# Attention and two gated layers on one core: a batch's sums inverted as 84 rows of 64 columns, re-laid through DRAM

## The chip, the cores and the metric

The kernel runs on one core of one Trainium2 chip. The metric is the time of one execution on the device, in microseconds (us). The engines are named as in the profile: PE (TensorE, matmuls; PEld are its weight loads), DVE (VectorE), ACT (ScalarE), POOL (GpSimd) and SP (SyncE, which issues nearly all DMAs, in the order of the program). A lower time is better.

## The reference

Attention over 4 batches of 12 heads, 448 positions and 64 columns a head, with scores capped by a tanh, and behind it two layers over 1792 tokens of 768 columns:

```python
scores = cap * np.tanh(scale * np.matmul(q, k.T) / cap)
attn = np.exp(scores - max);  attn = attn / (np.sum(attn, axis=-1) + 1e-09)
x = (attn @ v) as [B * S, H * D]
h = x @ w_in;   x = (h - np.tanh(h)) @ w_out
h = x @ w_in2;  x = (h / (1 + np.exp(-1.702 * h))) @ w_out2
```

The part that matters here is the division by the sums: 4 x 12 x 448 numbers are inverted, and each result multiplies 64 columns of a head's output.

## The kernel before

Attention takes the heads in pairs: 24 steps `g`, six to a batch. Keys lie on the partitions, so the sums over keys come from PE: `key_adds` adds a pair's key blocks on DVE, `sums_of_two` (L582) multiplies by a 0/1 matrix and leaves in a PSUM tile `ps_r` the sums of four heads, one row in each group of 32 partitions. `add_sums` (L605) collects three of them in an SBUF tile `w` of 128 partitions and 448 columns, of which 12 rows hold sums. In the two steps that follow, `batch_recip` (L610) inverts `w` in place, one half of the columns in a step, over all 128 partitions, and then stores the 12 rows to a DRAM tensor `wrow` (L615), which is in two parts, since the layers take the tokens in two passes (768 and 1024). `w_rows` (L621) loads a row again, repeated over 64 partitions, for the multiplication by the inverse: in the first pass as tiles `wb`, multiplied in attention (L666); in the second pass from DRAM in `x_load`, much later.

A step on PE is: two score blocks (L526), the transposes of a later pair's q and k (`prep`, L505 and L514, into two PSUM tiles `ps_qk`), the next pair's first score block, then in even steps `ps_r`, in odd ones the tails of two pairs, and the products with v (L568). `ps_qk` and `ps_r` share two PSUM buffers (`ps_s`), so `ps_r` starts only when DVE has copied the first of the two `ps_qk` out to `qk` (L90), and a transpose starts only when `add_sums` has read `ps_r`. The order of the work on PE, DVE, ACT and POOL in attention is that of the code (`pin`). DMAs are not pinned: a scheduler puts them between each other on SP. They are the loads of q, k and v (L465 to L493), the weights of the first layer (`wd`, L189), their converted parts to and from DRAM (`kept`, L240, L316), the part of attention's output that the second pass takes (`xd`, L592), `wrow` and `wb`.

Attention ends with the last batch's two reciprocals, while PE is already in the first layer's product (`gemm_in`, L912, a generator of which the end of attention takes the first matmuls). The last reciprocal and the last exponential are `marks`: some conversions of weights are placed behind them.

Of the kernel before, what the change touches and what calls it, by code (L numbers as in the profile page):

```python
# [9 lines left out]
F32 = mybir.dt.float32  # L10
# [5 lines left out]
ALU = mybir.AluOpType  # L16
# [24 lines left out]
def attention_moe_moe(ctx, tc, q, k, v, cap, w_in1, w_out1, w_in2, w_out2, out):  # L41
    nc = tc.nc
    B, H, S, D = q.shape
# [33 lines left out]
    def pin(ins):  # L77
        return tc.keep_in_program_order(ins) if pinned[0] else ins
# [13 lines left out]
    def lo_dve(dst, src, hi):  # L92
        return pin(nc.vector.tensor_tensor(out=dst, in0=src, in1=hi.bitcast(F32), op=ALU.subtract))  # L93

    ident = const.tile([P, P], F32, name="ident")
    make_identity(nc, ident)
    capr = const.tile([P, 1], F32, name="capr")
    cpos = const.tile([P, 1], F32, name="cpos")
    tsc = const.tile([P, 1], F32, name="tsc")
    cub_a = const.tile([P, 1], F32, name="cub_a")  # L100
    cub_u = const.tile([P, 1], F32, name="cub_u")
    const.tile([P, 24], F32, name="pad")

    xa = [dr_p.tile([P, TOKENS[0]], F32, name=f"xa{i}") for i in range(KM)]
    xd = [dr_p.tile([P, TOKENS[1]], F32, name=f"xd{i}") for i in range(KM)]
    wrow = [dr_p.tile([4, NP // 2, n], F32, name=f"wrow{p}") for p, n in enumerate(TOKENS)]
    x_big = big.tile([P, 2 * KM * TOKENS[0]], F32R, name="x")
    xs_h, xs_l = ([[x_big[:, (m * KM + i) * n:(m * KM + i + 1) * n] for i in range(KM)] for n in TOKENS[:1]] for m in range(2))
    xh, xl = list(xs_h[0]), list(xs_l[0])
# [17 lines left out]
    ps_v = first_pool("ps_v", 2, space=bass.MemoryType.PSUM)  # L127

    SR = P // 4
    sel = one_p.tile([P, NP // 2, SR], F32, name="sel")  # L130
    vt = [one_p.tile([P, P], F32, name=f"vt{i}") for i in range(4)]

# [316 lines left out]
    def parts_of(b):  # L449
        parts = []  # L450
        for p, n in enumerate(TOKENS):
            a, z = max(b * S - FIRST[p], 0), min((b + 1) * S - FIRST[p], n)
            if a < z:
                parts.append((p, a, z))
        return parts
# [142 lines left out]
    def add_sums(g):  # L598
        b, p = divmod(g // 2, NP // 2)
        ps = sum_t.pop(g)[:, :S]  # L600
        if p == 0:
            w_t[b] = w_p.tile([P, S], F32, tag="w", name="w")
            hi_dve(w_t[b], ps)
        else:
            pin(nc.vector.tensor_tensor(out=w_t[b], in0=w_t[b], in1=ps, op=ALU.add))  # L605

    def batch_recip(b, half):
        a = slice(half * S // 2, (half + 1) * S // 2)
        w = w_t[b]
        ins = pin(nc.vector.reciprocal(out=w[:, a], in_=w[:, a]))  # L610
        if half:
            c = 0
            for p, a, z in parts_of(b):
                for n in range(4):
                    nc.sync.dma_start(out=wrow[p][n, :, a:z], in_=w[n * SR:n * SR + NP // 2, c:c + z - a])  # L615
                c += z - a
        return ins

    def w_rows(t, p, i, a, z):
        for j in range(2):  # L620
            nc.sync.dma_start(  # L621
                out=t[j * D:(j + 1) * D], in_=wrow[p][i % 2 * 2 + j, i // 2, a:z].partition_broadcast(D)
            )

    conv_at = [3, 5, 7, 9, 11, 14, 16, 18, 20]
# [2 lines left out]
    def attention():  # L628
        wb = {}

        def x_of(g):
            return [n for n, at in enumerate(split_at) if at == g]

        def x_part(n):
            b, i = divmod(n, NP)
            n = S if b == 0 else CUT
            return i, n, slice(b * S, b * S + n)

        load_qk(0, nc.scalar)
        nc.sync.dma_start(out=capr, in_=cap.partition_broadcast(P))  # L640
        nc.vector.tensor_scalar(
            out=cpos.bitcast(U32), in0=capr.bitcast(U32), scalar1=0x7FFFFFFF, scalar2=None, op0=ALU.bitwise_and
        )
        nc.vector.reciprocal(out=tsc, in_=cpos)
        nc.vector.tensor_scalar(out=tsc, in0=tsc, scalar1=QK_SCALE, scalar2=None, op0=ALU.mult)
        load_qk(1)
        load_v(0)
        load_qk(2)
        load_v(1)

        def prep(g):
            prep_q(g)
            prep_k(g)

        prep(0)
        scores(0, 0)
        prep(1)
        tail_scores(0)
        for g in range(NG):
            pair_act(g, (0, KC) if g % 2 == 0 else (0,))  # L660
            if g - 2 in conv_at:
                conv_hi(early[conv_at.index(g - 2)])
            for n in x_of(g):
                i, w, a = x_part(n)
                x = xs[n][:, :w]
                pin(nc.vector.tensor_tensor(out=x, in0=x, in1=wb.pop(n)[:, :w], op=ALU.mult))  # L666
                hi_pool(xh[i][:, a], x)
            scores(g, 1)
            scores(g, 2)
            last_exp = pair_act(g, (1, 2))  # L670
            if g + 1 in conv_at:
                conv_exp(early[conv_at.index(g + 1)])
            load_v(g + 2)
            if g in conv_at:
                conv_low(early[conv_at.index(g)])
            if g - 1 in conv_at:
                conv_or(early[conv_at.index(g - 1)])
            for n in x_of(g):
                i, w, a = x_part(n)
                lo_pool(xl[i][:, a], xs.pop(n)[:, :w], xh[i][:, a])  # L680
            if g - 2 in conv_at:
                conv_lo(early[conv_at.index(g - 2)])
            if g >= NP and g % NP < 3:
                b = g // NP - 1
                if g % NP:
                    batch_recip(b, g % NP - 1)
            for n in {0: (2,), 1: (3, 4)}.get(g, (g + 3,)):
                prep(n)
            for n in {0: (3, 4)}.get(g, (g + 4,)):
                load_qk(n)  # L690
            for n in x_of(g + 1):
                wb[n] = wb_p.tile([P, S], F32, tag="wb", name="wb")
                i, w, a = x_part(n)
                w_rows(wb[n][:, :w], 0, i, a.start, a.stop)
            if g in (1, 3):
                dbl_dma()
            if g == NG - 1:
                tail_pv(g - 1)
                pair_pv(g, 0)
                prepare(1)  # L700
                hold[0] = True
                for _ in range(12):
                    next(moe_0)
            scores(g + 1, 0)
            if g % 2:
                tail_scores(g + 1)
                if g < NG - 1:
                    tail_pv(g - 1)
            elif g:
                sums_of_two(g - 2)  # L710
            key_adds(g)
            if g % 2 == 0 and g:
                add_sums(g - 2)
            for c in range(1 if g == NG - 1 else 0, KC):
                pair_pv(g, c)
            if g % 2:
                pair_out(g - 1)
                pair_out(g)
        for _ in range(5):
            next(moe_0)  # L720
        hold[0] = False
        sums_of_two(NG - 2)
        add_sums(NG - 2)
        for half in range(2):
            rec = batch_recip(B - 1, half)
        marks.extend((last_exp.ins, rec.ins))


    late = []
# [162 lines left out]

    def gemm_in(layer):
        for f in f_order[layer]:
            if plain[0] and f == KF - 1:
                rate[0] = 0.0
            i, (wh, wl) = w_next()
# [446 lines left out]
```

## Time and profile before

| | us |
|---|---|
| runs | 1053.99, 1056.22, 1056.51 |
| median | 1056.22 |
| profiled execution | 1055.68 |
| its span, first to last instruction | 1053.9 |
| PE busy in the span | 1038.7 |
| DVE busy | 819.6 |
| ACT busy | 692.0 |
| POOL busy | 56.1 |

The profile is of one execution. Its span leaves out 1.8 us around the instructions. Busy time of PE is modelled at the ends of matmuls. A row of the timeline begins with its start and its length in us; equal instructions that follow each other are one row with a count, and in brackets stands the engine's idle time before the row and what ended it. On SP a row's length is the time in which it issued the DMAs, not that of the transfers.

### The profile page before, as it was taken

What the parts mean: (1) busy time and instruction counts of PE and PEld (TensorE: products, weight loads), DVE (VectorE), ACT (ScalarE), POOL (GpSimd) and SP (SyncE); (2) the same over time, 40 slices, a digit from 0 to 9 for tenths busy, and PEclk for the clock granted to TensorE, in tenths of its full rate; (3) what the DMA queues carried; (4) which work ended last, traced back from release to release, by engine and by line L of the source; (5) the groups of instructions that cost most, each with busy time, mean ns of one, the idle gap of its engine ahead of it and who ended that gap; (6) DMA issues with size and microseconds to landing.
All of it is one profiled execution on the core that took longest, in us unless ns stands there. A gap on an engine that the chain in (4) does not pass through costs nothing.

```text
span 1053.9 us, 15397 instructions
## 1 busy us (share of the span) xinstructions
PE 1038.7 (99%) x5483; PEld 857.8 (81%) x5483; DVE 819.6 (78%) x1097; ACT 692.0 (66%) x958; POOL 56.1 (5%) x56
## 2 busy tenths in 40 slices
PE   8999999999999999999999999999999999999998
PEld 3333333899999998888878888887899999999998
DVE  4799999899986517988899897685899974448973
ACT  6999898787854335556775757655755745557663
POOL 0123444100000000000000000000000000000000
PEclk9999999999999999999999999999999999999999
DMA  5777688765588958888673852898654554444443
GB/s 132 196 217 219 181 228 257 255 228 192 195 257 275 327 170 287 289 277 283 219 253 118 299 183 82 272 321 297 224 164 126 190 155 130 129 118 143 153 134 104
DMA packets 153749, 218.17 MB, mean 207 GB/s; under 512 B 58380, under 2 KB 101704, under 8 KB 153672
## 3 DMA queue, kind: packets, MB, share of 16 engines
q1 hardware_dynamic: 152376, 216.58, 64.9%
q8 instruction: 43, 0.70, 0.3%
q10 hardware_dynamic: 1296, 0.61, 0.2%
q14 instruction: 34, 0.28, 0.1%
HBM read 158.86 MB, written 58.28 MB: 206 GB/s over the span
## 4 chain that ended last, share of the span: by engine, by line
PE 81%; DVE 11%; ACT 3%; DMA 3%; issue 2%; SPq 0%; DVEq 0%; ACTq 0%
PE ps_o L1194 19%; PE ps_h L912 19%; PE ps_h L1092 19%; PE ps_y L952 9%; PE ps_y L1005 5%; PE ps_pv L568 3%; PE ps_sc L526 3%; DVE gr L361 1%; DVE wl L93 1%; ACT t L545 1%; DVE rl L93 1%; DVE ts L557 1%; PE ps_r L582 1%; DVE ts L556 1%; PE ps_tl L536 1%
## 5 line engine op out<-in xcount | busy, mean ns | idle before, releaser
L81 ACT CAST rh<-gr 128x512 fp32r<-128x512 f32 (+1 forms) x179 | 103.6, 584 | 99.7 <-PE ps_o L1194 63.2
L912 PE MATMUL ps_h<-x,wh 128*128 128x384 f32 (+1 forms) x672 | 153.0, 358 | 0.0
L93 DVE TENSOR_TENSOR rl<-gr,rh 128x512 fp32r<-128x512 f32 (+1 forms) x179 | 113.8, 642 | 25.8 <-ACT rh L81 25.1
L1194 PE MATMUL ps_o<-wh,rl 128*128 128x384 f32 x392 | 131.1, 334 | 0.0
L1194 PE MATMUL ps_o<-wh,rh 128*128 128x384 f32 x392 | 131.1, 334 | 0.0
L1194 PE MATMUL ps_o<-wl,rh 128*128 128x384 f32 x392 | 131.1, 334 | 0.0
L912 PEld LDWEIGHTS ps_h<-x,wh 128*128 128x128 f32 x672 | 121.1, 188 | 12.0 <-issue 0.7
L93 DVE TENSOR_TENSOR wl<-whole,wh 128x768 fp32r<-128x768 f32 (+1 forms) x103 | 94.0, 912 | 13.7 <-ACT wh L81 12.8
L81 ACT CAST wh<-whole 128x768 fp32r<-128x768 f32 (+1 forms) x103 | 82.4, 800 | 24.7 <-PE ps_h L1092 10.6
L1092 PE MATMUL ps_h<-x,wh 128*128 128x384 f32 (+1 forms) x336 | 97.3, 359 | 0.0
L912 PE MATMUL ps_h<-x,wl 128*128 128x384 f32 (+1 forms) x384 | 88.1, 364 | 0.0
L545 ACT ACTIVATE t<-ps_sc,tsc 128x896 f32<-128x896 f32 x72 | 69.8, 1005 | 15.1 <-PE ps_sc L526 15.0
L912 PEld LDWEIGHTS ps_h<-x,wl 128*128 128x128 f32 x384 | 69.8, 188 | 9.7 <-issue 1.4
L1194 PEld LDWEIGHTS ps_o<-wl,rh 128*128 128x128 f32 x392 | 73.6, 188 | 0.0
L1194 PEld LDWEIGHTS ps_o<-wh,rh 128*128 128x128 f32 x392 | 73.6, 188 | 0.0
L1194 PEld LDWEIGHTS ps_o<-wh,rl 128*128 128x128 f32 x392 | 73.6, 188 | 0.0
L547 ACT ACTIVATE t<-t,cpos 128x896 f32<-128x896 f32 x72 | 72.4, 1042 | 0.4
L526 PE MATMUL ps_sc<-qk 64*128 64x448 f32 x288 | 68.3, 568 | 2.3 <-ACT t L545 1.5
L361 DVE TENSOR_TENSOR gr<-gr 128x512 f32<-128x512 f32 (+2 forms) x112 | 69.3, 645 | 0.6 <-DMA gr<-xa 0.4
L361 DVE TENSOR_TENSOR part<-ps_h,part 128x512 f32<-128x512 f32 (+1 forms) x48 | 29.8, 621 | 51.3 <-PE ps_h L1092 51.1
L1092 PE MATMUL ps_h<-x,wl 128*128 128x512 f32 (+1 forms) x192 | 69.6, 362 | 0.0
L219 DVE SCALAR_TENSOR_TENSOR wr<-wr,wd 128x768 uint32<-128x768 uint32 x48 | 46.0, 961 | 28.4 <-ACT wd L211 20.7
(155 smaller groups left out, 2188.1 us busy)
## 6 DMA issues: line engine op xcount, KB each, us to landing
wd<-in_moe_w_in_dram SPq DMA_DIRECT2D x64, 384.0 KB
wd<-in_moe_w_out_dram SPq DMA_DIRECT2D x29, 768.0 KB
whole<-single SPq DMA_DIRECT2D x36, 384.0 KB
whole<-s SPq DMA_DIRECT2D x33, 384.0 KB
wh<-kept SPq DMA_DIRECT2D x25, 384.0 KB
wl<-kept SPq DMA_DIRECT2D x25, 384.0 KB
single<-wr SPq DMA_DIRECT2D x24, 384.0 KB
whole<-t SPq DMA_DIRECT2D x22, 384.0 KB
```

The source lines that it names most:

```text
L81: pin(nc.scalar.copy(out=dst, in_=src))
L93: return pin(nc.vector.tensor_tensor(out=dst, in0=src, in1=hi.bitcast(F32), op=ALU.subtract))
L219: pin(nc.vector.scalar_tensor_tensor(out=u, in0=u, scalar=3, in1=dbls.pop(i)[:, :, 0], op0=ALU.logical_shift_left, op1=ALU.bitwise_or))
L361: nc.vector.tensor_tensor(out=out, in0=a, in1=b, op=kind)
L526: pin(nc.tensor.matmul(ps[:, j, :S], qk[a, kc], qk[a, :S], start=True, stop=True))
L545: pin(nc.scalar.activation(out=t, in_=ps[:, :, :S], func=AF.Tanh, scale=tsc))
L547: ins = pin(nc.scalar.activation(out=tt[g, c], in_=tt[g, c], func=AF.Exp, scale=cpos))
L912: pin(nc.tensor.matmul(ps, w[:, kk, :], x[kk][:, a], start=(m == 0), stop=(m == len(seq) - 1)))
L952: nc.tensor.matmul(bank[e][:, :a1 - a0], w[:, kk, c], x[2 * j + kk][:, a0:a1], start=(j == 0 and m == 0), stop=(j == KF // 2 - 1 and m == ...
L1005: nc.tensor.matmul(ps[e], w[:, kk, c], x, start=(name == head and k == 0 and m == 0), stop=(k == KH - 1 and m == 2), skip_group_check=True,)
L1092: nc.tensor.matmul(ps, w, x, start=(name == head and m == 0), stop=(m == len(seq) - 1), skip_group_check=True,)
L1194: nc.tensor.matmul(ps[n], x[:, t], w[:, kk, :], start=(first and k == 0 and m == 0), stop=(k == KH - 1 and m == 2), skip_group_check=True,)
```

## The change

The 12 rows of a batch's sums go to DRAM as they are (`wsum`, by `batch_store`, four stores as soon as the last sum is added), come back as a tile of 84 partitions and 64 columns (`batch_load`: partition c x 12 + r holds row r's columns 64 c to 64 c + 63), are inverted by one reciprocal and stored to `wrow` (`batch_recip`). In attention the load stands at the end of the step after the one with the last sum, and the reciprocal in the step after that, where the second half stood. The last batch's load and reciprocal move into `gemm_in`, at its chunks 4 and 6. `marks` now holds the last `add_sums`. The identity matrix moves to a pool that ends with attention, and `last_recip` takes a part of its room.

```diff
--- before.py
+++ after.py
@@ -92,18 +92,20 @@
     def lo_dve(dst, src, hi):
         return pin(nc.vector.tensor_tensor(out=dst, in0=src, in1=hi.bitcast(F32), op=ALU.subtract))
 
-    ident = const.tile([P, P], F32, name="ident")
-    make_identity(nc, ident)
     capr = const.tile([P, 1], F32, name="capr")
     cpos = const.tile([P, 1], F32, name="cpos")
     tsc = const.tile([P, 1], F32, name="tsc")
     cub_a = const.tile([P, 1], F32, name="cub_a")
     cub_u = const.tile([P, 1], F32, name="cub_u")
+    RW = 4 * (NP // 2)
+    WN = 64
+    last_recip = const.tile([RW * (S // WN), WN], F32, name="last_recip")
     const.tile([P, 24], F32, name="pad")
 
     xa = [dr_p.tile([P, TOKENS[0]], F32, name=f"xa{i}") for i in range(KM)]
     xd = [dr_p.tile([P, TOKENS[1]], F32, name=f"xd{i}") for i in range(KM)]
-    wrow = [dr_p.tile([4, NP // 2, n], F32, name=f"wrow{p}") for p, n in enumerate(TOKENS)]
+    wsum = [dr_p.tile([RW, S], F32, name=f"wsum{b}") for b in range(B)]
+    wrow = [dr_p.tile([RW, n], F32, name=f"wrow{p}") for p, n in enumerate(TOKENS)]
     x_big = big.tile([P, 2 * KM * TOKENS[0]], F32R, name="x")
     xs_h, xs_l = ([[x_big[:, (m * KM + i) * n:(m * KM + i + 1) * n] for i in range(KM)] for n in TOKENS[:1]] for m in range(2))
     xh, xl = list(xs_h[0]), list(xs_l[0])
@@ -127,6 +129,8 @@
     ps_v = first_pool("ps_v", 2, space=bass.MemoryType.PSUM)
 
     SR = P // 4
+    ident = one_p.tile([P, P], F32, name="ident")
+    make_identity(nc, ident)
     sel = one_p.tile([P, NP // 2, SR], F32, name="sel")
     vt = [one_p.tile([P, P], F32, name=f"vt{i}") for i in range(4)]
 
@@ -602,24 +606,36 @@
             w_t[b] = w_p.tile([P, S], F32, tag="w", name="w")
             hi_dve(w_t[b], ps)
         else:
-            pin(nc.vector.tensor_tensor(out=w_t[b], in0=w_t[b], in1=ps, op=ALU.add))
-
-    def batch_recip(b, half):
-        a = slice(half * S // 2, (half + 1) * S // 2)
-        w = w_t[b]
-        ins = pin(nc.vector.reciprocal(out=w[:, a], in_=w[:, a]))
-        if half:
-            c = 0
-            for p, a, z in parts_of(b):
-                for n in range(4):
-                    nc.sync.dma_start(out=wrow[p][n, :, a:z], in_=w[n * SR:n * SR + NP // 2, c:c + z - a])
-                c += z - a
-        return ins
+            ins = pin(nc.vector.tensor_tensor(out=w_t[b], in0=w_t[b], in1=ps, op=ALU.add))
+            if p == NP // 2 - 1:
+                batch_store(b)
+            return ins
+
+    recips = [one_p.tile([RW * (S // WN), WN], F32, name=f"recip{b}") for b in range(B - 1)] + [last_recip]
+
+    def rows_to_chunks(x):
+        return x.rearrange("r (c e) -> c r e", e=WN)
+
+    def batch_store(b):
+        w = w_t.pop(b)
+        for n in range(4):
+            nc.sync.dma_start(out=wsum[b][n * (NP // 2):(n + 1) * (NP // 2)], in_=w[n * SR:n * SR + NP // 2])
+
+    def batch_load(b):
+        nc.sync.dma_start(out=recips[b], in_=rows_to_chunks(wsum[b]))
+
+    def batch_recip(b):
+        pin(nc.vector.reciprocal(out=recips[b], in_=recips[b]))
+        c = 0
+        for p, a, z in parts_of(b):
+            n = RW * ((z - a) // WN)
+            nc.sync.dma_start(out=rows_to_chunks(wrow[p][:, a:z]), in_=recips[b][c:c + n])
+            c += n
 
     def w_rows(t, p, i, a, z):
         for j in range(2):
             nc.sync.dma_start(
-                out=t[j * D:(j + 1) * D], in_=wrow[p][i % 2 * 2 + j, i // 2, a:z].partition_broadcast(D)
+                out=t[j * D:(j + 1) * D], in_=wrow[p][(i % 2 * 2 + j) * (NP // 2) + i // 2, a:z].partition_broadcast(D)
             )
 
     conv_at = [3, 5, 7, 9, 11, 14, 16, 18, 20]
@@ -680,14 +696,14 @@
                 lo_pool(xl[i][:, a], xs.pop(n)[:, :w], xh[i][:, a])
             if g - 2 in conv_at:
                 conv_lo(early[conv_at.index(g - 2)])
-            if g >= NP and g % NP < 3:
-                b = g // NP - 1
-                if g % NP:
-                    batch_recip(b, g % NP - 1)
+            if g >= NP and g % NP == 2:
+                batch_recip(g // NP - 1)
             for n in {0: (2,), 1: (3, 4)}.get(g, (g + 3,)):
                 prep(n)
             for n in {0: (3, 4)}.get(g, (g + 4,)):
                 load_qk(n)
+            if g >= NP and g % NP == 1:
+                batch_load(g // NP - 1)
             for n in x_of(g + 1):
                 wb[n] = wb_p.tile([P, S], F32, tag="wb", name="wb")
                 i, w, a = x_part(n)
@@ -720,10 +736,7 @@
             next(moe_0)
         hold[0] = False
         sums_of_two(NG - 2)
-        add_sums(NG - 2)
-        for half in range(2):
-            rec = batch_recip(B - 1, half)
-        marks.extend((last_exp.ins, rec.ins))
+        marks.extend((last_exp.ins, add_sums(NG - 2).ins))
 
 
     late = []
@@ -892,6 +905,8 @@
 
     def gemm_in(layer):
         for f in f_order[layer]:
+            if not plain[0] and f in (4, 6):
+                (batch_load if f == 4 else batch_recip)(B - 1)
             if plain[0] and f == KF - 1:
                 rate[0] = 0.0
             i, (wh, wl) = w_next()
```

Where the scheduler puts the new DMAs shows in the order of SP. First for batch 1 (`wsum_95`), about step 13; `kept` and `wb` are as above. Before:

```order
L240 DMA kept_148<-wl 128x768
L465 DMA raw<-in_q_dram 112x4x64 x2
L489 DMA rv<-in_v_dram 128x2x192
L471 DMA raw<-in_k_dram 128x3x64 x2
L475 DMA raw<-in_k_dram 64x2x64
L465 DMA raw<-in_q_dram 112x4x64 x2
L471 DMA raw<-in_k_dram 128x3x64 x2
```

And now:

```order
L244 DMA kept_153<-wl 128x768
L469 DMA raw<-in_q_dram 112x4x64 x2
L622 DMA wsum_95<-w 3x448 x4
L493 DMA rv<-in_v_dram 128x2x192
L475 DMA raw<-in_k_dram 128x3x64 x2
L625 DMA recip_260<-wsum_95 84x1x64
L479 DMA raw<-in_k_dram 64x2x64
L469 DMA raw<-in_q_dram 112x4x64 x2
```

The four stores stand behind the q loads, and the load three DMAs behind them. For batch 2 (`wsum_96`), about step 19, SP had before:

```order
L240 DMA kept_152<-wl 128x768
L489 DMA rv<-in_v_dram 128x2x192
L189 DMA wd<-in_moe_w_in_dram 128x3x256 x2
L240 DMA kept_154<-wh 128x768
L240 DMA kept_154<-wl 128x768
```

And now:

```order
L244 DMA kept_157<-wl 128x768
L493 DMA rv<-in_v_dram 128x2x192
L622 DMA wsum_96<-w 3x448 x4
L193 DMA wd<-in_moe_w_in_dram 128x3x256 x2
L625 DMA recip_261<-wsum_96 84x1x64
L244 DMA kept_159<-wh 128x768
L244 DMA kept_159<-wl 128x768
```

Here two loads of weights stand between the stores and the load. On DVE the same place of batch 1 was before:

```order
L605 TENSOR_TENSOR w<-w,ps_r 128x448
L610 RECIPROCAL w<-w 128x224
L90 COPY qk<-ps_qk 128x448 x2
L556 TENSOR_TENSOR ts<-t 128x896
L557 TENSOR_TENSOR ts<-ts,tl 64x896
L558 TENSOR_TENSOR ts<-ts,t 128x896
L90 COPY xs<-ps_pv 128x448 x2
L666 TENSOR_TENSOR xs<-xs,wb 128x448
L213 TENSOR_SCALAR wd<-wd 128x768
L610 RECIPROCAL w<-w 128x224
L90 COPY qk<-ps_qk 128x448 x2
```

And now:

```order
L609 TENSOR_TENSOR w<-w,ps_r 128x448
L90 COPY qk<-ps_qk 128x448 x2
L560 TENSOR_TENSOR ts<-t 128x896
L561 TENSOR_TENSOR ts<-ts,tl 64x896
L562 TENSOR_TENSOR ts<-ts,t 128x896
L90 COPY xs<-ps_pv 128x448 x2
L682 TENSOR_TENSOR xs<-xs,wb 128x448
L217 TENSOR_SCALAR wd<-wd 128x768
L628 RECIPROCAL recip_260<-recip_260 84x64
L90 COPY qk<-ps_qk 128x448 x2
```

The first half is gone; the new reciprocal stands where the second half stood, ahead of the copies of `qk`.

## Rows read from the trace of the kernel before

**Rows 1.** The page's head: span, and busy time, share and instructions.

```profile
span 1053.9 us, 15397 instructions
PE 1038.7 (99%) x5483; PEld 857.8 (81%) x5483; DVE 819.6 (78%) x1097; ACT 692.0 (66%) x958; POOL 56.1 (5%) x56
```

**Rows 2.** Busy time by stretches: length, engines (instructions), clock, DMA share, GB/s.

```profile
154.00:171.00 17.00, 15.23 (x92) 6.01 (x92) 16.59 (x20) 14.34 (x16) 2.66 (x2) 1.00 0.89 278
...
186.00:200.00 14.00, 14.00 (x83) 10.16 (x82) 11.11 (x14) 8.77 (x12) 2.05 (x1) 1.00 0.63 208
200.00:300.00 100.00, 100.00 (x579) 100.00 (x578) 92.30 (x106) 83.40 (x105) 0.00 (x0) 1.00 0.63 213
```

**Rows 3.** PE's waits: total us, times, longest.

```profile
PE ps_r L582 <- DVE qk L90: 2.8, 4, 1.2
PE ps_qk L514 <- DVE w L605: 1.8, 2, 1.2
```

**Rows 4.** Timeline of DVE and PE around the first three batches' reciprocals.

```profile
73.04 1.55 DVE L610 RECIPROCAL w<-w 128x224 f32<-128x224 f32 x1
...
75.12 0.96 PE L582 MATMUL ps_r<-ts,sel 128*32 128x448 f32 x8 [0.23 <-DVE qk L90]
...
111.08 0.61 DVE L605 TENSOR_TENSOR w<-w,ps_r 128x448 f32<-128x448 f32 x1
...
119.58 1.54 DVE L610 RECIPROCAL w<-w 128x224 f32<-128x224 f32 x1
...
121.66 0.96 PE L582 MATMUL ps_r<-ts,sel 128*32 128x448 f32 x8 [0.71 <-DVE qk L90]
...
156.26 0.61 DVE L605 TENSOR_TENSOR w<-w,ps_r 128x448 f32<-128x448 f32 x1
...
165.26 1.55 DVE L610 RECIPROCAL w<-w 128x224 f32<-128x224 f32 x1
...
167.34 0.96 PE L582 MATMUL ps_r<-ts,sel 128*32 128x448 f32 x8 [1.21 <-DVE qk L90]
```

**Rows 5.** Groups by line: busy us, mean ns, idle before.

```profile
L610 DVE RECIPROCAL w<-w 128x224 f32<-128x224 f32 x8 | 12.2, 1539 | 0.0
```

**Rows 6.** Timeline of SP about batch 0.

```profile
66.39 1.49 SPq L471 DMA_DIRECT2D raw<-in_k_dram  x2
...
76.71 1.29 SPq L615 DMA_DIRECT2D wrow<-w  x4
...
81.29 1.13 SPq L621 DMA_DIRECT2D wb<-wrow  x2
```

**Rows 7.** Timeline of SP about batch 1.

```profile
114.09 2.42 SPq L465 DMA_DIRECT2D raw<-in_q_dram  x2
116.61 0.64 SPq L489 DMA_DIRECT2D rv<-in_v_dram  x1
117.31 1.25 SPq L471 DMA_DIRECT2D raw<-in_k_dram  x2
118.60 0.62 SPq L475 DMA_DIRECT2D raw<-in_k_dram  x1
...
126.38 2.50 SPq L615 DMA_DIRECT2D wrow<-w  x8
128.93 1.12 SPq L621 DMA_DIRECT2D wb<-wrow  x2
```

**Rows 8.** Timeline: the load of cap on SP and what waits for it.

```profile
2.27 0.80 SPq L640 DMA_DIRECT2D capr<-in_cap_dram  x1
...
5.52 0.15 DVE L641 TENSOR_SCALAR cpos<-capr 128x1 uint32<-128x1 uint32 x1 [4.38 <-DMA capr<-in_cap_dram]
```

**Rows 9.** Timeline of SP about batch 2.

```profile
162.88 0.39 SPq L489 DMA_DIRECT2D rv<-in_v_dram  x1
163.37 1.16 SPq L189 DMA_DIRECT2D wd<-in_moe_w_in_dram  x2
```

## The prediction

> **What bounds the kernel now.** Read first the page's head: in a span of 1053.9 us TensorE (PE) is busy 99% [rows 1]. So VectorE (DVE) time counts only where PE stands waiting for DVE, and I look at the attention stage, where the change sits, for such places. The table by stretches [rows 2] shows two kinds of stretch: in 154 to 171 us PE is busy 15.23 of 17.00 us and DVE 16.59, so DVE sets the pace there; in 186 to 200 and 200 to 300 us PE has no gap at all. The reader is to see that a DVE saving can pay only before 186 us. Then the list of PE's waits [rows 3]: the sum matmul (ps_r) waited 2.8 us in 4 places for the copies of qk, and a transpose 1.8 us in 2 places for the add into w. Third, the timeline around the reciprocals [rows 4]. At the second half of each of the first three batches the order on DVE is reciprocal, copies of qk, and ps_r waits for the first copy: its wait is 0.23 us (75.12), 0.71 us (121.66) and 1.21 us (167.34). The fourth of the 4 places has no reciprocal near, and the two waits for w are ahead of the first halves (111.08 and 156.26 are adds that come late by themselves); so these stay.
>
> **What is removed.** Eight reciprocals of 128x224 at 1539 ns, 12.2 us of DVE [rows 5]. What PE can get back is bounded by its waits behind them: 0.23 + 0.71 + 1.21 = 2.15 us. The first halves of three batches have no PE wait behind them: there the step hides them. The last two, at the end of attention, run beside a PE that is busy 14.00 of 14.00 us [rows 2]: worth 0. Without that cover they would be worth 3.1 us; as there is no gap at all, I don't count on any of it.
>
> **What is added on DVE.** Four reciprocals of 84x64. In proportion to columns one is 1539 x 64 / 224 = 0.44 us; a whole old one, 1.54 us, is the upper end. I take 0.5 us, near the lower end, since it is the same operation on the same engine; what part of 1539 ns is fixed no row shows. From a reciprocal's end to the start of ps_r it is 119.58 + 1.54 to 121.66, that is 0.54 us [rows 4]. So after the change ps_r starts 0.5 + 0.54 = 1.04 us after the new reciprocal can start.
>
> **What is added on the queue.** SyncE (SP) issues the DMAs in the order of the program. Removed are 20 stores (4, 8, 4 and 4), added 16 stores of w, 4 loads and 5 stores of the inverse: 5 more. Old stores took 1.29 us for 4 and 2.50 for 8, about 0.32 each [rows 6, 7]; I price the new stores of w at that and a load at 0.5, as the broadcast loads (1.12 for 2). What matters is not their sum but that DVE now waits for SP: the reciprocal stands in DVE's order ahead of the copies of qk, and if its load has not landed, the copies wait, and ps_r and all of PE behind them. Before, nothing on DVE at this place waited for SP.
>
> How late is SP? Very. For batch 1 the reciprocal ended at 121.12 but its stores were issued only at 126.38 [rows 4, 7]: SP was some 5 us behind, and the rows of that group follow each other with hardly a gap. That is my reason to expect the load late.
>
> How long from an issue to what it feeds? Stores first: at 126.38 eight went out, of which the first four feed the load at 128.93; the fourth was issued at about 126.38 + 3 x 0.32 = 127.34, so it had landed within 1.6 us. At 76.71 the fourth of four was issued near 77.7, and the load that needs it at 81.29: 3.6 us, a load of weights being ahead [rows 6]. I take the middle, 2.6. For a load's landing the trace has one small one with its end: cap, issued at 2.27, let DVE start at 5.52, 3.25 us [rows 8]. I take 3.25; the ends are 1.6 (the quick store) and 4.58 (76.71 to 81.29, the slow store counted from its first issue).
>
> *Batch 1.* New order on SP: q loads, four stores, v, two k, then the load. The q loads ended at 114.09 + 2.42 = 116.51; four stores make it 117.8, v (116.61 to 117.31) 118.5, k (117.31 to 118.60) 119.8. The stores, the last issued at 117.5, have landed at 119.1 to 121.1, middle 120.1. So the load goes at 119.8 / 120.1 / 121.1 and lands at 121.4 / 123.35 / 125.7. DVE wanted to start it at 119.58. ps_r comes at 122.4 / 124.4 / 126.7 against 121.66: 0.8, 2.7 or 5.1 us lost, where 0.71 was to be gained.
>
> *Batch 2.* New order: v, four stores, two weight loads, then the load [rows 9]. v ended at 163.27, stores 164.6, weights (1.16) 165.8; the last store, issued at 164.3, has landed at 165.9 / 166.9 / 167.9. The load lands at 167.5 / 170.15 / 172.5. SP itself is later than before by what is added and removed up to here: two groups of four stores and a load (2 x 1.8) less 3 and 6 old stores (9 x 0.32 = 2.9), 0.7 us. In the middle ps_r comes at 170.15 + 0.7 + 1.04 = 171.9 against 167.34.
>
> *Batch 0.* k loads end at 67.88; stores 69.2, v and the k tail 70.5 (0.6 and 0.7 as later in the queue), one q 71.15. Last store landed at 70.5 to 72.5, load landed at 72.8 to 77.1; DVE wants to start at 73.04. ps_r: between the full gain of 0.23 and 3.0 us lost; no weight burst stands in front here as in rows 7 and 9, so I take the quick side: 0.
>
> **The sum.** SP does not wait for PE where it is behind, so its clock fixes batch 2, and what batch 1 loses is inside what batch 2 shows, not beside it: 171.9 - 167.34 = 4.6 us by then. After it PE has no gap to give it back (200 to 300 us: 100.00 of 100.00). Low end +1.2 (167.5 + 1.04 - 167.34), high end +6.9 (172.5 + 0.7 + 1.04 - 167.34). The profiled execution took 1055.68: 1060.3. The runs shown have their median 0.54 above it, so I say 1060.6.
>
> *The last batch.* Its load and reciprocal lie in the first layer behind the fifth and seventh chunk. DVE is busy 92.30 of 100 us there and PE 100 [rows 2]; behind the reciprocal wait the activation's own steps, which PE needs only in the second product. Cost 0; if the load came after DVE reached it, at most the same 3.25 us of DVE, which the three pairs of banks ahead of PE would take up in part.
>
> The order of the small operations at the seam also changes (the first chunk's subtraction comes after two weight conversions): hidden by the same full PE.
>
> Here the Trainium skill bears on both sides. The rows above show a dependent load issued 1.6 to 3.6 us after its store [rows 6, 7]. "DMA: Bandwidth & Descriptors", section "Two DMAs through the same engine are not ordered", says that a dependent DMA has to be held back on the issuing engine until the first one's semaphore is complete: SP then stands still with everything behind it, and the rows agree, for at 81.29 it did. The same page, "Anatomy of one DMA", gives about 2 us of fixed cost per DMA; by that, an estimate, store and load make 4 us, less than a step, and the result would be the first rival's.
>
> **Rivals.**
> 1. *The loads are in time: faster.* The adds into w end at 111.7 and 156.9, and DVE wants the reciprocals at 119.58 and 165.26, 7.9 and 8.4 us later [rows 4]. Store and load by the middle values are 2.6 + 3.25 = 5.9 us. If SP issued both at once, all 2.15 us would come back: 1055.68 - 2.15 + 0.54 = 1054.1. Against it: in batch 1 SP reaches the stores 4.8 us after the add. It decides from a landing before 119.58.
> 2. *A small loss.* Low ends above: +1.2, 1057.4. For it: the q loads' 2.42 us hold a stall of the queue that could shrink; the lateness of SP would then be less.
> 3. *A second wait.* The broadcast rows of batch 0 are loaded at 81.29 and used soon after; SP is 1.8 us later there (four stores and a load). If the multiply on DVE then waits too, up to 1.8 us come on top where SP does not hide them: with the high end, 1062 to 1064.
> 4. *The change does not do what it says.* If 64 columns cost as much as 224 (1.54 us, the upper end above), the reciprocals that PE waits behind are as long as before; only the first halves and the last pair go, which PE does not feel: 1055.68 + 0.54, no change, if the loads are in time too.
>
> **Chances.** Forecast 0.45; rival 1 0.15; rivals 2 and 4 0.25; rival 3 0.15. 0.3% is 3.2 us, about what a measurement tells from no change here: faster means under 1053.1, slower above 1059.4. Rival 1 reaches under 1053.1 only with something more: 0.10 faster. Rivals 2 and 4, the rest of rival 1 and the forecast's lower part make 0.35 the same. The rest, 0.55, is slower. The range 1054 to 1064.5 leaves out the best of rival 1 and the worst of rival 3; the forecast's own is 1057.4 to 1063.1.
>
> **What would show it.** In the profile after: DVE idle before RECIPROCAL, released by the DMA of the load, 3 to 4 us at batch 1 and some at batch 2; PE's waits of ps_r for qk grown from 2.8 to 6 us or more; reciprocals of 0.44 to 0.6 us; PE still without a gap from 200 us on. I am wrong if DVE does not wait there, or if SP has reached the load before DVE's turn.

## The result, and the profile after

The changed kernel takes 1067.08 us (median of 6 runs, 1065.34 to 1069.95) beside 1055.78 for the kernel before in the same comparison: a ratio of 1.0111, 95% interval 1.0092 to 1.0129. It is slower, as forecast, but by 11.3 us instead of 4.4, and outside the range of 1054 to 1064.5. The profiled execution took 1067.76, 12.08 more than that of before.

The head of the page after: the span, then busy time of each engine.

```profile
span 1065.9 us, 15405 instructions
...
PE 1042.1 (98%) x5483; PEld 858.4 (81%) x5483; DVE 810.9 (76%) x1093; ACT 692.0 (65%) x958; POOL 53.6 (5%) x56
```

DVE did lose 8.7 us of work [rows 1]. PE has gained gaps and, for the same instructions, 3.4 us of busy time. The waits (total us, times, longest) and the reciprocals by line:

```profile
PE ps_r L586 <- DVE qk L90: 11.7, 5, 6.8
DVE recip L628 <- DMA recip<-wsum: 11.7, 3, 7.5
DVE xs L682 <- DMA wb<-wrow: 1.1, 1, 1.1
```

```profile
L628 DVE RECIPROCAL recip<-recip 84x64 f32<-84x64 f32 x3 | 1.6, 549 | 11.7 <-DMA recip<-wsum 11.7
```

A reciprocal is short, 549 ns, but three of them waited 11.7 us in all for their load, and PE's wait of `ps_r` behind the copies of qk rose from 2.8 [rows 3] to 11.7. Batch 1 on SP, DVE and PE, in order of start:

```profile
117.66 2.47 SPq L469 DMA_DIRECT2D raw<-in_q_dram  x2
120.22 1.92 SPq L622 DMA_DIRECT2D wsum<-w  x4
...
123.78 1.25 SPq L475 DMA_DIRECT2D raw<-in_k_dram  x2
125.21 0.88 SPq L625 DMA_DIRECT2D recip<-wsum  x1
...
127.62 0.55 DVE L628 RECIPROCAL recip<-recip 84x64 f32<-84x64 f32 x1 [7.55 <-DMA recip<-wsum]
...
128.71 1.72 PE L586 MATMUL ps_r<-ts,sel 128*32 128x448 f32 x8 [6.80 <-DVE qk L90]
...
130.36 4.20 PE L572 MATMUL ps_pv<-t,rv 128*64 128x448 f32 x12
```

And batch 2:

```profile
169.65 0.39 SPq L493 DMA_DIRECT2D rv<-in_v_dram  x1
170.13 1.42 SPq L622 DMA_DIRECT2D wsum<-w  x4
...
173.67 0.88 SPq L625 DMA_DIRECT2D recip<-wsum  x1
...
177.06 0.55 DVE L628 RECIPROCAL recip<-recip 84x64 f32<-84x64 f32 x1 [3.02 <-DMA recip<-wsum]
...
178.15 1.67 PE L586 MATMUL ps_r<-ts,sel 128*32 128x448 f32 x8 [3.15 <-DVE qk L90]
179.75 3.41 PE L572 MATMUL ps_pv<-t,rv 128*64 128x448 f32 x12
```

Two things are to be seen. The load is issued late (125.21, 173.67), and all behind it on DVE and PE waits in a row. And after the wait the same matmuls are slower: `ps_r` takes 1.72 and 1.67 us where it took 0.96 [rows 4]. The table by stretches says why (the columns are length, PE, PEld, DVE, ACT and POOL busy, granted clock, DMA share, GB/s):

```profile
121.00:127.00 6.00, 0.91 (x5) 0.18 (x4) 0.00 (x0) 4.03 (x5) 0.70 (x1) 1.00 0.66 192
127.00:131.00 4.00, 2.29 (x10) 0.50 (x12) 3.34 (x5) 0.00 (x0) 0.00 (x0) 0.51 0.45 101
131.00:134.00 3.00, 3.00 (x10) 0.93 (x8) 2.90 (x5) 0.00 (x0) 0.38 (x1) 0.52 0.63 168
178.00:182.00 4.00, 3.85 (x16) 1.07 (x18) 3.86 (x6) 0.46 (x1) 0.00 (x0) 0.57 0.69 211
200.00:300.00 100.00, 100.00 (x576) 97.31 (x575) 89.04 (x102) 81.00 (x102) 0.00 (x0) 1.00 0.64 216
```

PE stood nearly still from 121 to 127 us, and in the 7 us behind that its granted clock was 0.51 and 0.52, the lower level (1.2 GHz). So the sum of the loss can be read off. With 2.48 us for twelve `ps_pv` at full clock (a row of the fourth experiment shows it), batch 1 lost 6.80 - 0.71 = 6.09 by the wait, 1.72 - 0.96 = 0.76 and 4.20 - 2.48 = 1.72 by the clock; batch 2 lost 3.15 - 1.21 = 1.94, 0.71 and 0.93. That makes 12.15, for 12.08 between the two profiled executions. From 200 to 300 us PE has no gap, as before [rows 2].

The last thing is where SP's lateness begins. Batch 0:

```profile
79.41 0.84 SPq L632 DMA_DIRECT2D wrow<-recip  x1
...
80.84 0.38 SPq L244 DMA_DIRECT2D kept<-wl  x1
83.58 2.02 SPq L637 DMA_DIRECT2D wb<-wrow  x2
```

The stores of the inverse go 2.70 us later than before (76.71 [rows 6]), since the new stores and the load stand ahead of them. SP then stands from 81.22 to 83.58, as the broadcast loads have to wait for that store (they go 4.17 us after its issue, 4.58 before); SP's own list of waits has it:

```profile
SPq L637 <- DMA wrow<-recip: 2.3, 1, 2.3
```

The two issues of the broadcast loads take 2.02 us for 1.13: they end at 85.60 against 82.42, 3.18 late. From there to the q loads of batch 1 no gap between SP's rows is above 0.4 us, and these come at 117.66 against 114.09 [rows 7]: 3.57 late. What SP loses at batch 0 it still owes at batch 1. By batch 2 it owes more: the load of v just ahead of the stores comes at 169.65 against 162.88 [rows 9], 6.77 late.

### The profile page after: what moved, and what is told of

It reads as the page before. It is cut to its first block, busy times and chain, and to the rows that moved or that the text cites. A ratio compares the mean times of both kernels' runs of the same rounds, so it can differ in the third digit from the quotient of the medians.

```text
span 1065.9 us, 15405 instructions
## 1 busy us (share of the span) xinstructions
PE 1042.1 (98%) x5483; PEld 858.4 (81%) x5483; DVE 810.9 (76%) x1093; ACT 692.0 (65%) x958; POOL 53.6 (5%) x56
## 4 chain that ended last, share of the span: by engine, by line
PE 75%; DVE 9%; DMA 8%; ACT 3%; issue 3%; SPq 2%; DVEq 0%; ACTq 0%
PE ps_o L1209 19%; PE ps_h L927 16%; PE ps_h L1107 16%; PE ps_y L967 9%; PE ps_y L1020 4%; PE ps_pv L572 4%; PE ps_sc L530 3%; DVE wl L93 2%; DMA wd<-in_moe_w_in_dram 1%; DVE gr L365 1%; DMA wd<-in_moe_w_out_dram 1%; DVE rl L93 1%; PE ps_r L586 1%; PE ps_tl L540 1%; DMA s<-wr 1%
```

## The experiments

Theory A: SP is the bound of this stage in the changed kernel. It is late by what the change adds to its queue, the lateness is carried from batch to batch, and DVE's reciprocal is only the place where PE meets it. Theory B: the place in DVE's order, ahead of the copies of qk, makes the loss. Theory C: the last batch, at the seam between attention and the first layer, costs something. Theory D: the clock's fall is the part that the forecast lacked. The expectations below have letters of their own; "its A" and "its B" are those of the expectation just above. Each kernel was compared with before on the same chip; the medians of before lay between 1056.33 and 1056.67.

**1. The load without its wait.**

```diff
-        nc.sync.dma_start(out=recips[b], in_=rows_to_chunks(wsum[b]))
+        nc.sync.dma_start(out=landed[b], in_=rows_to_chunks(wsum[b]))
```

> The stores, the loads and the small reciprocals of batches 0 to 2 stay where they are, but the load lands in a tile of its own and the reciprocal works on a tile of ones, so DVE has no load to wait for (the inverse of these batches is left out of the result). Theory A (DVE waits for a load that SP issues too late, and PE with it): steps 14 and 20 go back from 16.23 and 11.74 us to about 6.9 and 6.9 to 7.6, with the 0.8 and 1.3 us of the old reciprocal gone too, so 13 to 14 us under the changed kernel: 1053 to 1055. Theory B (the five more DMAs make SP late for everything, and PE pays for that): no wait of DVE's reciprocal, but the time stays above 1062.

Measured: 1060.75, ratio 1.0052 (1.0026 to 1.0077), between its two theories. The reciprocals wait no longer, but SP's lateness shows two steps later, at the broadcast rows of batch 1 (timeline of DVE and PE):

```profile
138.07 0.49 DVE L686 TENSOR_TENSOR xs<-xs,wb 128x320 f32<-128x320 f32 x1 [4.49 <-DMA wb<-wrow]
139.62 1.37 PE L586 MATMUL ps_r<-ts,sel 128*32 128x448 f32 x8 [3.66 <-DVE qk L90]
```

So some 4 to 5 of the 11 us need no wait of the reciprocal at all: another wait stands behind it in the row.

**2. Stores and loads of the sums on POOL's queue.**

```diff
-            nc.sync.dma_start(out=wsum[b][...], in_=w[...])
+            nc.gpsimd.dma_start(out=wsum[b][...], in_=w[...])
...
-        nc.sync.dma_start(out=recips[b], in_=rows_to_chunks(wsum[b]))
+        nc.gpsimd.dma_start(out=recips[b], in_=rows_to_chunks(wsum[b]))
```

> All four batches' stores of sums and loads are issued by POOL instead of SP; nothing else changes. Theory A, with the cause in SP's order (loads behind q, k and weights that SP has not issued yet): the stores go within 1 us of the add into w, the loads land within about 6 us, before DVE's turn some 7.9 us after the add, and the time is 1053 to 1056. If the cause is not the place in SP's order but the transfers behind which a small DMA lands (they share the DMA engines), the loads land as late as before relative to the add, and the time stays above 1060.

Measured: 1060.36, ratio 1.0038 (1.0021 to 1.0055). This is outside the band of 1053 to 1056. The stores did go within 1 us of the add, but the loads landed some 10 us after it and not 6: at batch 1 the add ended at 111.30, and the reciprocal started at 122.14. The waits for the load shrink to 2.8 us in two places, 2.03 the longest. Five DMAs a batch off SP give back more than half. The profiled execution took 1056.40, 4 us under the median, so where the rest is lost its trace does not show.

**3. Only the last batch through DRAM.** Batches 0 to 2 keep the two half reciprocals.

```diff
-            if p == NP // 2 - 1:
+            if b == B - 1 and p == NP // 2 - 1:
                 batch_store(b)
...
-            if g >= NP and g % NP == 2:
-                batch_recip(g // NP - 1)
+            if g >= NP and 0 < g % NP < 3:
+                half_recip(g // NP - 1, g % NP - 1)
...
```

The cut parts are `half_recip`, which does what `batch_recip` did before, and the loads of these batches, which go.

> Batches 0 to 2 are inverted in halves in place as before the change; only the last batch takes the way through DRAM, with its load and reciprocal in the first layer. Theory A: nothing at the seam waits, so the time is that of the kernel before within 1 us: 1055 to 1057. Theory C (the moved marks and the new order at the seam cost part of the 11 us): 1058 or more.

Measured: 1056.77, ratio 1.0006 (0.9990 to 1.0022). No cost of the seam shows, and the interval leaves room for 2 us at most; theory C does not explain the loss.

**4. Keep PE busy while it waits.** Zero products ahead of `ps_r`, 30 at batch 1 and 15 at batch 2.

```diff
+                for _ in range({14: 30, 20: 15}.get(g, 0)):
+                    pin(nc.tensor.matmul(ps_pv(g), wz[:, :P], wz, start=True, stop=True, skip_group_check=True))
                 sums_of_two(g - 2)
```

> The changed kernel with 30 matmuls of zeros of 512 columns in step 14 and 15 in step 20, put before the sum matmul, so that PE works while it would wait (about 6.4 and 3.2 us at 0.213 each). Theory D: of the 8.6 and 3.6 us of these steps, 2.5 and 1.6 are not wait but the half clock that the profile shows after it (ps_r 1.72 and 1.67 us against 0.96, the products with v 4.20 and 3.41 against 2.48); with PE busy the clock stays at 1.00, and 3 to 4 us come back: 1063 to 1064. If the clock is not set by the wait, the time is 1067 or more.

Measured: 1068.62, ratio 1.0129 (1.0109 to 1.0148): no gain. PE at batch 1, then SP, DVE and PE at batch 2:

```profile
129.25 0.96 PE L586 MATMUL ps_r<-ts,sel 128*32 128x448 f32 x8
130.14 2.48 PE L572 MATMUL ps_pv<-t,rv 128*64 128x448 f32 x12
...
175.06 0.88 SPq L625 DMA_DIRECT2D recip<-wsum  x1
177.95 0.55 DVE L628 RECIPROCAL recip<-recip 84x64 f32<-84x64 f32 x1 [5.86 <-DMA recip<-wsum]
179.03 1.01 PE L586 MATMUL ps_r<-ts,sel 128*32 128x448 f32 x8 [2.64 <-DVE qk L90]
179.97 4.07 PE L572 MATMUL ps_pv<-t,rv 128*64 128x448 f32 x12
```

At batch 1 the clock held, and the 2.48 us came back. But the load of batch 2 did not come sooner for that (175.06, after 173.67), and the wait there grew from 3.02 to 5.86 us. What PE wins at batch 1 it waits for at batch 2, where SP sets the time. So theory D is right about that step and wrong about the total. At batch 2 the clock fell all the same behind the shorter row of zero products (4.07 us for the twelve `ps_pv`).

**5. The reciprocal a step later.**

```diff
-    split_at = [10, 11, 12, 14, 15, 21, 16, 17, 18, 21, 22, 22]
+    split_at = [11, 12, 13, 14, 15, 21, 17, 18, 19, 21, 22, 22]
...
-            if g >= NP and g % NP == 2:
+            if g >= NP and g % NP == 3:
```

> The small reciprocals of batches 0 to 2 stand one step later (fourth step of the next batch, not the third), and the products that need the first broadcast rows of batches 0 and 1 a step later too; stores and loads stay on SP. Theory A (the loss is DVE arriving at the reciprocal before its load has landed, some 7.5 us too early at batch 1 and 3.0 at batch 2; a step is 6.9 to 7.7 us): the waits for the load fall from 11.7 to under 2 us, ps_r does not wait long enough for the clock to fall, and the time is 1053 to 1057. Theory B (SP has simply too much to do here, and its lateness reaches PE by one wait or the other): other waits, for the broadcast rows, take the place: 1059 to 1064. Rival C (the clock alone): no clock drop, but waits as before: about 1063.

Measured: 1063.31, ratio 1.0071 (1.0055 to 1.0088). No reciprocal waits, but DVE waits 5.25, 2.75 and 3.67 us for broadcast rows, and PE 2.28 us for a load of k:

```profile
DVE xs L682 <- DMA wb<-wrow: 11.7, 3, 5.3
```

These are the "other waits" of its B, which is theory A of this section.

**6. The reciprocal behind the copies of qk.**

```diff
+            for n in {0: (2,), 1: (3, 4)}.get(g, (g + 3,)):
+                prep(n)
             if g >= NP and g % NP == 2:
                 batch_recip(g // NP - 1)
-            for n in {0: (2,), 1: (3, 4)}.get(g, (g + 3,)):
-                prep(n)
```

> The change as it is, but in DVE's order the small reciprocals of batches 0 to 2 stand behind the two copies of qk instead of ahead of them; SP's order is that of the change. Theory A (the loss comes from the copies of qk being held behind a reciprocal that waits): ps_r's wait falls from 11.7 to under 2 us at the three places; DVE still waits 3 to 7 us for the load, but now in front of the key additions, which PE needs only a step later, so that one part of it comes back: 1056 to 1061. Theory B (SP's lateness decides, wherever DVE waits for it): the wait only moves to another PE line, 1064 or more. [...]

Measured: 1063.12, ratio 1.0070 (1.0052 to 1.0087), above the band of its A and below that of its B. The waits of the profiled execution, which took 1065.66:

```profile
DVE xs L682 <- DMA wb<-wrow: 8.2, 2, 5.0
PE ps_r L586 <- DVE qk L90: 7.6, 2, 4.2
DVE recip L628 <- DMA recip<-wsum: 4.0, 3, 2.3
```

At the three reciprocals `ps_r` does not wait any more, as its A has it; the two waits that are left stand elsewhere, behind broadcast rows. So theory B holds for some 4 us, the difference to the change; the rest of the loss moved.

**7. The same order in the kernel before**, the half reciprocals behind the copies; nothing is added.

```diff
+            for n in {0: (2,), 1: (3, 4)}.get(g, (g + 3,)):
+                prep(n)
             if g >= NP and g % NP < 3:
...
                     batch_recip(b, g % NP - 1)
-            for n in {0: (2,), 1: (3, 4)}.get(g, (g + 3,)):
-                prep(n)
```

> The kernel before with one edit: its half reciprocals stand behind the two copies of qk in DVE's order instead of ahead of them. This measures the gain that was bounded to 2.15 us by PE's waits behind the reciprocals (0.23 + 0.71 + 1.21 us), without any DMA added. Theory: these waits of ps_r go, and the time falls by 1.0 to 2.2 us, to 1054.3 to 1055.5. Rival: DVE sets the pace in that stretch (it is busy 16.59 of 17.00 us), so the waits only move behind the copies: within 0.5 us of before.

Measured: 1061.85, ratio 1.0050 (1.0031 to 1.0068), outside both expectations. At batch 1 `ps_r` waits for nothing now, as wanted; but the stores of the inverse go later, at 78.68 for 76.71 [rows 6] and at 131.58 for 126.38 [rows 7], and with them the broadcast rows (timeline of SP and DVE):

```profile
131.58 2.63 SPq L615 DMA_DIRECT2D wrow<-w  x8
...
136.46 0.49 SPq L621 DMA_DIRECT2D wb<-wrow  x1
...
140.89 0.49 DVE L666 TENSOR_TENSOR xs<-xs,wb 128x320 f32<-128x320 f32 x1 [5.87 <-DMA wb<-wrow]
```

The kernel before has no reserve on SP: with its stores 2 us later from batch 0 on, it lost 5.5.

**8. Batch 0's products a step later**, so that SP need not stand for the stores.

```diff
-    split_at = [10, 11, 12, 14, 15, 21, 16, 17, 18, 21, 22, 22]
+    split_at = [11, 12, 13, 14, 15, 21, 16, 17, 18, 21, 22, 22]
```

> The change with one number moved: the first three products of batch 0 with the broadcast rows stand a step later (11, 12, 13 instead of 10, 11, 12), so SP need not stand still for the stores of the inverse (81.22 to 83.58 us in the trace of the change) and for the slow broadcast load behind it (2.02 us). Theory A (what SP loses at batch 0 is carried, with no gap in its queue, to batch 1): SP reaches the q loads of batch 1 2 to 3 us earlier than 117.66, the wait of ps_r there falls from 6.80 to 3.5 to 5 us, total 1062 to 1065. Theory B (each batch's wait has its own cause): batch 1's wait stays at 6 to 7 us, 1066 to 1068.

Measured: 1067.19, ratio 1.0101 (1.0081 to 1.0121). The total and the wait at batch 1 came as its B has them, a miss for its A, but not for B's reason. The carrying is there: the q loads come at 114.69, 2.97 earlier than 117.66, and batch 1's `ps_r` at 125.74, 2.97 earlier than 128.71. But PE had come 2.4 us earlier too, so its wait was still 6.24; and at batch 2 the load went at 173.28, the wait grew to 5.98, and all was given back, as in the fourth experiment. The waits hang together, through SP.

**9. The loads of v on POOL**, from the seventh pair on: other work off SP, the change as it is.

```diff
-        nc.sync.dma_start(
+        (nc.gpsimd if g > 5 else nc.sync).dma_start(
             out=tv.rearrange("p h c d -> p h (c d)"),
```

The same for the tail rows of v.

> The change as it is, but the loads of v from the seventh pair on are issued by GpSimd (POOL, 5% busy) instead of SyncE: 3 issues of each step, some 2 us, leave SP's queue. Theory A (SP is the bound of the stretch from 75 to 180 us: each wait, for the sums' load, for the broadcast rows or for k, is SP being late): SP reaches the loads of batches 1 and 2 in time, the waits of ps_r for the copies of qk fall from 11.7 to about 2 us, the clock stays, and the time is 1053 to 1057. Theory B (the chain store, load, reciprocal, store, load is too long by itself, however early SP is): DVE still waits 3 us or more for the load at batches 1 and 2, 1060 or more. Rival C: v comes late, since POOL waits for DVE's products: PE waits for rv instead.

Measured: 1054.90 (1052.76 to 1056.89, 12 runs), ratio 0.9983 (0.9972 to 0.9994): faster than both kernels. Batches 1 and 2 in its timeline:

```profile
117.59 0.86 SPq L625 DMA_DIRECT2D recip<-wsum  x1
120.00 0.55 DVE L628 RECIPROCAL recip<-recip 84x64 f32<-84x64 f32 x1 [0.28 <-DMA recip<-wsum]
121.48 0.96 PE L586 MATMUL ps_r<-ts,sel 128*32 128x448 f32 x8
...
158.96 0.89 SPq L625 DMA_DIRECT2D recip<-wsum  x1
164.95 0.54 DVE L628 RECIPROCAL recip<-recip 84x64 f32<-84x64 f32 x1
166.02 0.96 PE L586 MATMUL ps_r<-ts,sel 128*32 128x448 f32 x8 [0.26 <-DVE qk L90]
```

The loads go 7.6 and 14.7 us earlier than in the change and are there in time, the clock does not fall, and PE's wait at `ps_r` is 0.9 us in all where before had 2.8 [rows 3]: 1.9 of the 2.15 us that could be won. From the one load to the next SP takes 41.4 us here, with a stand of 2.5 us in which it waits for the sums: it is no longer behind. This is the first rival's course, and it needs SP's relief. The Trainium skill, "DMA: Bandwidth & Descriptors", section "Issuing engines are not separate DMA queues", says that a second issuing engine saves only the sequencer's time to start a DMA, "which is usually small relative to the DMA itself". These runs agree that it is issue time that is saved; here it is what decides.

**10. The same move in the kernel before.**

```diff
-        nc.sync.dma_start(
+        (nc.gpsimd if g > 5 else nc.sync).dma_start(
             out=tv.rearrange("p h c d -> p h (c d)"),
```

> The kernel before with the same move: loads of v from the seventh pair on are issued by POOL. Theory A (SP's lateness costs the kernel before almost nothing, it only leaves no reserve): 1055.5 to 1057, the same; PE's 2.15 us behind the reciprocals and 1.8 us behind the additions stay, as they are DVE's. If it is over 1 us faster, the kernel before lost time to SP too; if slower, POOL's queue has a price of its own that the run of the change with the same move holds as well.

Measured: 1059.26, ratio 1.0023 (1.0008 to 1.0038), slower, the last of the three cases. So the move by itself is no gain. With v on POOL the change is worth 1054.90 - 1059.26 = -4.4 us. In the trace `ps_r` waits 2.46 us behind batch 2's second half reciprocal and takes 1.72 us at the lower clock; but the profiled execution took 1055.99, 3.3 us under the median, so it does not show the loss. Why POOL's issues cost the kernel before something stays open.

**11. Only the stores of xd on POOL.**

```diff
-                nc.sync.dma_start(out=xd[i][:, a:z], in_=x[:, S - (z - a):])
+                nc.gpsimd.dma_start(out=xd[i][:, a:z], in_=x[:, S - (z - a):])
```

> The change, with only the stores of xd (two for each two steps, 0.42 to 0.55 us each on SP) issued by POOL. Theory A (SP's own issue time sets when the loads of the sums go, and each us taken off its queue comes back): up to batch 1's load 6 issues leave, 2.9 us, up to batch 2's 12, 5.8 us. The load of batch 1 is issued near 122.3 instead of 125.21, that of batch 2 near 168 instead of 173.67, and the time falls by about 5.8 us, to 1060 to 1063. Theory B (not the time to issue, but landings that SP waits for, hold the queue): the loads move by less than 2 us, 1065 to 1068.

Measured: 1064.75, ratio 1.0076 (1.0058 to 1.0095), between its two bands: less came back than its A said. The loads moved as its A has it, and a little further (timeline of SP and PE at batches 1 and 2):

```profile
121.04 0.88 SPq L625 DMA_DIRECT2D recip<-wsum  x1
...
124.43 1.55 PE L586 MATMUL ps_r<-ts,sel 128*32 128x448 f32 x8 [3.83 <-DVE qk L90]
...
166.41 0.88 SPq L625 DMA_DIRECT2D recip<-wsum  x1
...
171.09 0.96 PE L586 MATMUL ps_r<-ts,sel 128*32 128x448 f32 x8
```

4.2 and 7.3 us earlier; batch 2 no longer makes PE wait. The profiled execution (1063.00) is 4.8 us below that of the change. In attention it won more; from the last step's first scores to the end it took 873.0 us, the change 869.1, before 869.6 and the ninth experiment 871.0. What makes this stretch differ is not shown.

**12. v on POOL only up to batch 1.**

```diff
-        (nc.gpsimd if g > 5 else nc.sync).dma_start(
+        (nc.gpsimd if 5 < g < 15 else nc.sync).dma_start(
```

> As the run with v on POOL, but only for the seventh to fifteenth pair, that is up to batch 1's reciprocal; from then on v is SP's again. Theory A (SP has about 48.5 us of work for one batch of the change, from 125.21 to 173.67, where PE needs about 45, and waits for nothing): batch 1's load goes as early as with v on POOL throughout, 117.6, without a wait; batch 2's load goes near 166 and lands near 168.5, so that DVE waits 2 to 4 us there and the time is 1057 to 1060. Theory B (only the first stand at batch 0 matters): both are in time, as with v on POOL throughout: 1053 to 1056.

Measured: 1059.27, ratio 1.0028 (1.0009 to 1.0046), inside the band of its A. Batch 1 is in time, and batch 2 is late again (timeline of SP and DVE):

```profile
116.30 0.88 SPq L625 DMA_DIRECT2D recip<-wsum  x1
118.74 0.54 DVE L628 RECIPROCAL recip<-recip 84x64 f32<-84x64 f32 x1
...
163.30 0.88 SPq L625 DMA_DIRECT2D recip<-wsum  x1
166.62 0.55 DVE L628 RECIPROCAL recip<-recip 84x64 f32<-84x64 f32 x1 [2.75 <-DMA recip<-wsum]
```

From one load to the next SP takes 47.0 us here, 48.5 in the change, 49.9 and 51.0 in the fourth and eighth experiments, 45.4 in the eleventh and 41.4 in the ninth. PE does the six steps from 117.01 to 161.20 here, in 44.2, so a lead that SP is given at batch 1 is used up by batch 2; only the ninth experiment has SP faster than PE.

Together: theory A holds. Less work on SP brings the loads forward (experiments 9, 11, 12), and with enough of it the whole loss goes, while the same move gains nothing in the kernel before. An edit that leaves SP's work as it is (4 to 6, 8) gives back 4 us at most, and even the one that drops the wait for the loads (1) only 6.

## Where the prediction was right, and where it failed

**Right: the place and the chain.** DVE idle before the reciprocal, released by the load, with the copies of qk and `ps_r` behind it, at batches 1 and 2. At batch 0 DVE waited 1.15 us for the load, and `ps_r` came as before (at 75.10 after a wait of 0.22, against 0.23 [rows 4]). The reciprocal: 0.5 said, 0.549 measured. From its start to `ps_r`: 1.04 said, 1.09 measured (127.62 to 128.71). From the stores to the reciprocal: 5.9 us in the middle, 5.48 and 5.51 measured from the end of the four stores' issue (122.14 and 171.55), with other issues of SP in between. The 4 us that the text sets against them are worked out from a figure that the Trainium skill ("DMA: Bandwidth & Descriptors", "Anatomy of one DMA") gives for DMAs that GpSimd issues. For these of SP it was low: a store of the inverse was waited for until 4.17 us after its issue, and the loads landed 2.38 to 3.39 us after theirs. The last batch's cost of 0: the third experiment shows none. The 2.15 us that could be won: 1.9 came back once the loads were in time.

**Failed: "SP itself is later than before ... 0.7 us".** This is the term that put the time outside the range. The middle had batch 2's load issued at 166.9 + 0.7 = 167.6; it went at 173.67, 6.1 late. All of this is SP's lateness ahead of the stores: the load of v before them was 6.77 late and not 0.7, while from that load to the load of the sums the text has 4.0 us (162.88 to 166.9), and 4.02 were measured (169.65 to 173.67). The landing made up nothing (3.39 for 3.25), so `ps_r` came at 178.15 for 171.9. What the runs showed in place of the 0.7:
- *Batch 0's delay, left out for batch 1.* The text has SP 1.8 us later at the broadcast rows of batch 0, but only as a price in the third rival; batch 1's working starts from the unchanged 114.09 + 2.42. As nothing in SP's rows lets it catch up, the 3.57 us belonged into every later step. Added to the 124.4 of batch 1 they make 128.0; measured was 128.71, with the load issued 1.5 us later still and landing 0.8 us faster.
- *A count of issues is no time on a full queue.* Old and new issues were weighed against each other (3.6 less 2.9 us). Four stores took 1.92 us at batch 1 and not 1.3, v and two k from 122.14 to 125.03, 2.9 for 2.0, as SP also stood in between. The two broadcast loads of batch 0 took 2.02 for 1.13.

**Failed, smaller: no clock in the sum.** The clock's fall behind the stalls, 2.48 and 1.64 us, is in no term. By the fourth experiment the first is hidden, since SP sets batch 2's time; the second came on top.

**Held, though it looks otherwise: "what batch 1 loses is inside what batch 2 shows".** In the profile the two waits add up to the loss. But where batch 1's part was made smaller, by the clock or by an earlier SP, batch 2's grew by as much, twice. What has to be relieved is SP, over the whole stage. The *landing* of 3.25 us, taken from one load of another kind, was too long at batches 0 and 1 (2.38 and 2.41, the latter from 125.21 to 127.62); that it fitted at batch 2 is luck.

**The rivals.** The first was right that the loads can be in time, and the ninth experiment shows on what condition: an SP that is not behind. The third, the wait for the broadcast rows, came as 1.15 us in the change and as the main wait in experiments 1, 5, 6 and 7: its mechanism is real, and the first wait hides it. The second is out: the q loads, whose 2.42 us were to shrink, took 2.47. The fourth is out by 549 ns.

## What to carry to other kernels

Where one queue issues nearly everything and its rows follow each other without a gap, keep its lateness as a running account: add what each edit costs at the first place where it stands, and carry it to all later ones. On such a queue a wait that is removed shows the next one, so relieve the queue instead of moving its consumer. An edit that looks good on the compute engines can lose on such a queue and gain once other issues go to an idle engine: 11.3 us lost here, 1.7 won with the loads of v on POOL.

## What the runs showed of the hardware that was not expected

- PE's granted clock fell to the lower level behind waits of 6.80, 3.15 and, in the tenth experiment, 2.46 us, with eight `ps_r` at 1.72, 1.67 and 1.72 us instead of 0.96. Behind a wait of 2.86 us in the twelfth it fell too, but a little later: the `ps_r` behind the wait ran at full clock, and the twelve `ps_pv` after it took 4.17 us instead of 2.48 (timeline of PE):

```profile
167.71 0.96 PE L586 MATMUL ps_r<-ts,sel 128*32 128x448 f32 x8 [2.86 <-DVE qk L90]
168.60 4.17 PE L572 MATMUL ps_pv<-t,rv 128*64 128x448 f32 x12
```

So full speed in the first matmuls behind a wait does not say that the clock held. In the second experiment it stayed at the upper level behind a wait of 2.18 us. What decides was not tried.
- A reciprocal of 64 columns takes 549 ns, one of 224 columns 1539 [rows 5]: by the difference of the two an estimate of 6.2 ns for each further column and some 150 ns besides (84 and 128 partitions, taken as alike).
- The kernel before has a cliff beside it: half reciprocals moved by about 2 us (73.04 to 75.12 at batch 0) cost 5.5 us, through the DMAs behind them.
